# Attention transposes two row blocks behind their scores, seven probability buffers, and the memory features written over the query rows

## Chip, core and metric

The kernel runs on one core of one Trainium2 chip, as one launch. The metric is the device time of that launch in microseconds (us). An engine that a row names PE is TensorE's matmuls, PEld its weight loads, DVE VectorE, ACT ScalarE, POOL GpSimd and SP the engine that only issues transfers here.

## The reference

Three steps run one after the other. Attention has 4 batches, 8 heads, 576 rows and 64 columns per head; the feed-forward steps see 2304 rows of 512.

```python
scores = scale * np.matmul(q, k.transpose(0, 1, 3, 2))
scores = np.where(causal, -1000000000.0, scores)
scores = scores - scores.max(-1, keepdims=True)
a = np.exp(scores)
a /= a.sum(-1, keepdims=True) + 1e-09
local = np.matmul(a, v)
def phi(x):
    return np.where(x > 0, x, np.exp(x) - 1.0) + 1.0
q_p = phi(q)
mem_ret = np.einsum('bhsd,bhde->bhse', q_p, M_prev)
mem_norm = np.einsum('bhsd,bhd->bhs', q_p, z_prev)[..., None] + 1e-06
out = g * mem_ret / mem_norm + (1 - g) * local     # g = sigmoid(beta), one per head
x = ((x @ w1) * (x @ w2)) @ w3 @ w_out             # x: heads side by side, d_ff 1024
y = (sigmoid(x @ w_gate) * (x @ w_val)) @ w_out2   # d_ff 1536
```

## The kernel before, in words

**Attention.** `attention(b, lag)` (L1066) is a generator for one batch. The 576 rows are cut into five blocks of 116, the eight heads into four pairs; step k of its main loop is row block i of pair p, with p, i = k // 5, k % 5. For each step, `s_part` has TensorE multiply a query block with all keys up to the diagonal, for both heads of the pair (L1169; in batches 1 to 3 three matmuls each, over the high and low parts that `split_qk` makes of q and k), and DVE reads the scores out of PSUM, adds the mask and keeps the row extremum (L1174). Block 4 has 580 columns, more than a PSUM bank holds, so it is done in two pieces: the tiles `s{b}_{p}_4_0_*` and `s{b}_{p}_4_1_*`. The pool for scores has two buffers, one for each head, so the matmuls of the second piece wait until DVE has read the first. Then ACT takes the exponential (`e_part`, L137), DVE and POOL scale the rows (`n_part`, L1197 to L1200), and `t_part` has TensorE transpose the finished block `p` (L1230) into PSUM, from where ACT copies it to `pt` or `pq` (L1248). When the five blocks of a pair are transposed, `a_part` multiplies them with v and adds the memory term (L1283 to L1298), and `l_part` copies the result out.

**The memory term.** `load_rest(p)` loads a pair's query rows `qnr` (L1093, 128 x 640), z, v and M. `mem_steps(p)` makes phi of them on DVE, ACT and POOL: `me` = min(q, 0) (L1107), its exponential, phi = max(q + 1, e) into a tile `mphi` (L1110), the product with z, its row sums and their reciprocal (L1112 to L1117), and phi times that (L1121). `qt_part(p)`, called in block 3 of the pair, has TensorE transpose the result (L1267). `load_rest(p + 1)` is called in block 4 of pair p, and `mem_steps(p + 1)` starts with the next pair.

**The lag.** Step k of the loop also asks for the transposes of step k - lag. In batch 0 the lag is LAG0 = 3, in batches 1 to 3 it is LAG. The probability tiles `p` have PB buffers, two of which one step takes. Transposes of blocks 2 and 3 and the first part of block 4, the q transposes and the output of `a_part` share one PSUM buffer (pool `ps_o`, 1024 columns) in batches 1 to 3.

**The feed-forward steps** (`ffn(b)`) fill TensorE between these: names `ab`, `xw`, `gv`, `abp`, `gvp`, `ot` are their outputs in PSUM, `h`, `hg`, `x` their inputs, and `wslot` is a ring of five weight buffers, which SP fills (L450, L453). `drive()` advances the two generators in proportion to their work; attention of batch b + 1 runs beside the feed-forward steps of batch b. Weights are prepared on chip (products, and high and low parts: `wraw`, `wrawl`, `wS`, `wP`), with loads and stores on the same SP queue.

**What sets the order.** From the feed-forward steps on, TensorE's order is that in which the code issues it. DVE, ACT, POOL and SP are ordered ahead of time by a scheduler that simulates the program; each engine then works through its own list in order, and waits where a row's inputs or buffers are not ready.

Of the kernel before, what the change touches and what calls it, by code (L numbers as in the profile page):

```python
# [7 lines left out]
F32 = mybir.dt.float32  # L8
# [10 lines left out]
B, H, S, D = 4, 8, 576, 64  # L19
T = 116  # L20
NT = 5
# [7 lines left out]
F2 = 1536 // 128  # L29
NJ = F1 + F2  # L30
LAG0 = 3
LAG = 1
PB = 5
RING = 5
R64 = 3
P0 = 8
# [27 lines left out]
def tile_attention_memory_ffn(  # L64
# [21 lines left out]
    ap = ctx.enter_context(tc.tile_pool(name="ap", bufs=2))  # L86
# [24 lines left out]
    def lower(share):  # L111
        owed[share] = owed.get(share, 0.0) + share[phase["n"]]
        if owed[share] >= 1.0:
            owed[share] -= 1.0
            return nc.gpsimd
        return nc.vector
# [19 lines left out]
    def act_fn(**kw):  # L136
        ins = nc.scalar.activation(**kw)  # L137
        if act_last:
            tc.add_manual_dep(
                ins.ins,  # L140
                act_last.pop(),
                mybir.DependencyInfo(mybir.DependencyClass.NoSync, mybir.DependencyReason.DATA),
                reason="table order",
            )
        act_last.append(ins.ins.name)
# [221 lines left out]
    def load64(n):  # L367
        if n < len(conv_slots):
            s = conv_slots[n]
            t = fp.tile([128, 512], I64, tag="r64", name=f"r64_{s}", bufs=R64)  # L370
            src = units[s // 2][0][s % 2]
            d = nc.sync.dma_start(out=t, in_=src.rearrange("p a c -> p (a c)"))
            raw64[s] = t
            last["dma"] = d
# [691 lines left out]
    def attention(b, lag):  # L1066
# [22 lines left out]

        def load_rest(p):  # L1090
            if p < NPAIR:
                q_ = ap.tile([128, NT, 2, D], F32, tag="qnr", name=f"qnr{b}_{p}")
                nc.sync.dma_start(out=q_, in_=qn[b, p])  # L1093
                z_ = ap.tile([128, 2, D], F32, tag="z", name=f"z{b}_{p}")
                nc.sync.dma_start(out=z_, in_=zb[b, p])
                v_ = ap.tile([128, NT, 2, D], F32, tag="vs", name=f"vs{b}_{p}")
                nc.sync.dma_start(out=v_, in_=vn[b, p])
                m_ = ap.tile([128, D], F32, tag="ms", name=f"ms{b}_{p}")
                nc.sync.dma_start(out=m_, in_=md[b, p])
                pairs[p] = (q_[:T], v_[:T], m_, z_[:T])  # L1100

        def mem_steps(p):
            q_, _, _, z_ = pairs[p]
            e = ap.tile([T, NT, 2, D], F32, tag="me", name=f"me{b}_{p}", bufs=1)
            phi = ap.tile([T, NT, 2, D], F32, tag="mphi", name=f"mphi{b}_{p}", bufs=1)
            nrm = ap.tile([T, NT, 2], F32, tag="mn", name=f"mn{b}_{p}", bufs=1)
            nc.vector.tensor_scalar(e, q_, 0.0, None, ALU.min)  # L1107
            yield
            act_fn(out=e, in_=e, func=AF.Exp)
            nc.vector.scalar_tensor_tensor(phi, q_, 1.0, e, ALU.add, ALU.max)  # L1110
            yield
            nc.gpsimd.tensor_mul(e, phi, z_.unsqueeze(1).to_broadcast([T, NT, 2, D]))  # L1112
            yield
            nc.vector.tensor_reduce(nrm, e, AX.X, ALU.add)
            nc.vector.tensor_scalar(nrm, nrm, 1e-6, None, ALU.add)
            nc.vector.reciprocal(nrm, nrm)
            nc.vector.tensor_mul(  # L1117
                nrm, nrm, g[:T, 2 * p : 2 * p + 2].unsqueeze(1).to_broadcast([T, NT, 2])
            )
            yield  # L1120
            lower(SHARE_M).tensor_mul(phi, phi, nrm.unsqueeze(3).to_broadcast([T, NT, 2, D]))  # L1121
            qms[p] = phi


        load_qk(0)
        yield 0.0
        load_rest(0)
        yield 0.0 if first else 0.5
        if first:
# [16 lines left out]
        def s_part(p, i, n):  # L1146
            w = T * (i + 1)
            if n == 0:
                ps_ = []
                for hh in range(2):  # L1150
# [4 lines left out]
                    else:  # L1155
                        ps_.append(ap.tile([T, SP], F32, tag="p", name=name, bufs=PB))
                    np_["n"] += 1
# [175 lines left out]
        for k in range(NPAIR * NT + lag):  # L1333
# [3 lines left out]
            if k < NPAIR * NT:  # L1337
                p, i = divmod(k, NT)
                wgt = 0.25 + 0.25 * (i + 1)
                s_part(p, i, 0)  # L1340
                yield wgt
                if i == NT - 1:
                    s_part(p, i, 1)
                    yield 0.0
                if i == 0:
                    mem = mem_steps(p)
                next(mem, None)
                e_part(p, i, 0)
                yield wgt + between(kk % NT)
                e_part(p, i, 1)  # L1350
                yield wgt + between(kk % NT)
                n_part(p, i)
                if i > 0:
                    next(mem, None)
                if i == 3:
                    qt_part(p)
                if i == 0:
                    load_qk(p + 2 if first else p + 1)
                if i == 4:
                    split_qk(p + 1)  # L1360
                if i == 4:
                    load_rest(p + 1)
                yield wgt + between(kk % NT)
                yield wgt + between(kk % NT)
                yield wgt + between(kk % NT)
            while ts:
                yield ts.pop(0)()
            if kk >= 0 and kk % NT == NT - 1:
                p = kk // NT
# [6 lines left out]
    def drive(fg, ag, ftot, atot, frac, most=1):  # L1376
        fd = ad = 0.0
        alive = ag is not None
        for c in fg:
            fd += c  # L1380
            for _ in range(most):
                if not alive or ad / atot >= fd / (ftot * frac):
                    break
                with tc.high_priority(offset=AHEAD[phase["n"]]):
                    w = next(ag, None)
                if w is None:
                    alive = False
                else:
                    ad += w
        while alive:  # L1390
            alive = next(ag, None) is not None
# [16 lines left out]
    def start():  # L1408
        for g in range(NPREP):
            yield from prep(g)  # L1410
# [3 lines left out]
    def chain(first, second):  # L1414
        for c in first:
            if c is not READY:
                yield c
        if second is not None:
            while True:
                if phase["n"] == 0:  # L1420
                    with tc.issue_after(last["dma"].ins):
                        c = next(second)
                else:
                    c = next(second)
                if c is READY:
                    return
                yield c

    a0 = attention(0, LAG0)
    with tc.manual_schedule(engines={mybir.EngineType.SP}):  # L1430
# [6 lines left out]
        for n in range(2, R64):  # L1437
            load64(n)
    atts = [a0] + [attention(b, LAG) for b in range(1, B)] + [None]
    drive(start(), chain(a0, atts[1]), 42.4 * NPREP + 8 * WAIT, ATOT, 1.0, most=9)  # L1440
# [80 lines left out]
```

## Time and profile before

| | us |
|---|---|
| median of 3 runs | 1017.32 |
| lowest and highest | 1014.89 and 1017.90 |
| the profiled execution | 1013.13 |
| its span on the core | 1011.3 |

The profiled execution is 1.8 us longer than its span and 4.2 us shorter than the median. In the rows below, each engine's busy time is followed by its share of the span. A row of waits says which engine waited at which line for what, the total in us, how often, and the longest. A row of a timeline gives the start in us from the start of the span, how long, the instruction, how many of them in a row, and in brackets the idle time ahead of it with what ended that. "Idle before" in the groups of instructions is the same, summed.

### The profile page before, as it was taken

The page shows a single profiled execution, that of the slowest core. Times are in us where ns is not written, and L with a number is a line of the kernel's source. Part 1 is how long each engine was busy: PE and PEld are TensorE (multiplying, and loading weights), DVE is VectorE, ACT ScalarE, POOL GpSimd, SP SyncE. Part 2 cuts the span into 40 slices and gives each one's busy share as a digit, 9 for nine tenths or more (in the row PEclk, how much of TensorE's full clock was granted, in tenths as well). Part 3 has the DMA queues.
Part 4 walks back from the last instruction along what each step waited for, and adds up shares of the span by engine and source line. Part 5 has one row for each costly group of instructions (what it writes and reads, how often), then busy time and mean ns, then how long its engine had stood idle before and what let it go on. Part 6 is the DMA issues. An engine that isn't in the chain of part 4 may idle for free. (4 is left out here: it accounts for less than half of the span.)

```text
span 1011.3 us, 19894 instructions
## 1 busy us (share of the span) xinstructions
PE 982.4 (97%) x7351; PEld 797.9 (79%) x7351; DVE 731.3 (72%) x1702; ACT 596.6 (59%) x1213; POOL 195.0 (19%) x196
## 2 busy tenths in 40 slices
PE   7999999999999999999999999999999999999998
PEld 3556687888999898898977777778777667797776
DVE  6866788777778826777777668988876757737883
ACT  7987787567777735564654545555655545324451
POOL 3454012213000101312200011343111311201110
PEclk9989999999999999999999999999999999999999
DMA  8865799967777249877887576655655556556532
GB/s 293 245 230 192 247 346 310 326 206 254 249 250 247 98 137 380 286 226 238 297 310 261 176 251 240 214 190 184 200 181 178 185 157 204 186 174 246 183 131 79
DMA packets 95642, 227.21 MB, mean 225 GB/s; under 512 B 11192, under 2 KB 39992, under 8 KB 95288
## 3 DMA queue, kind: packets, MB, share of 16 engines
q1 hardware_dynamic: 95544, 225.93, 66.3%
q8 instruction: 58, 0.95, 0.4%
q14 instruction: 40, 0.33, 0.1%
HBM read 164.55 MB, written 61.34 MB: 223 GB/s over the span
## 5 line engine op out<-in xcount | busy, mean ns | idle before, releaser
L532 PEld LDWEIGHTS <-wslot 128*128 128x128 f16 x1680 | 162.9, 98 | 49.7 <-issue 8.3
L1200 POOL TENSOR_SCALAR p<-p,sm,omg 116x116 f32<-116x116 f32 (+4 forms) x100 | 89.0, 895 | 406.2 <-DVE sm L1198 294.9
L521 PE MATMUL gv<-x,wslot 128*128 128x288 f32 (+1 forms) x1152 | 147.5, 290 | 0.2 <-ACT gsb L137 0.2
L521 PEld LDWEIGHTS <-wslot 128*128 128x128 f16 x1152 | 111.1, 98 | 32.1 <-issue 4.5
L532 PE MATMUL gvp<-x,wslot 128*128 128x288 f16 x1008 | 125.2, 286 | 3.6 <-ACT x L180 1.6
L137 ACT ACTIVATE p<-p,sm 116x116 f32<-116x116 f32 (+4 forms) x160 | 93.2, 585 | 46.6 <-DVE sm L1174 46.5
L521 PE MATMUL ot<-hg,wslot 128*128 128x288 f16 (+1 forms) x864 | 118.1, 291 | 0.0
L521 PE MATMUL ab<-x,wslot 128*128 128x288 f32 x768 | 117.2, 302 | 0.5 <-ACT asb L800 0.3
L521 PE MATMUL xw<-h,wslot 128*128 128x288 f32 x768 | 113.0, 300 | 1.7 <-ACT h L721 1.0
L521 PEld LDWEIGHTS ab<-x,wslot 128*128 128x128 f32 x768 | 104.0, 188 | 6.3 <-issue 2.9
L521 PEld LDWEIGHTS xw<-h,wslot 128*128 128x128 f32 x768 | 103.4, 188 | 5.5 <-issue 2.0
L1174 DVE CUSTOM_DVE_ANT_0 p<-s,msk 116x116 f32<-116x116 f32 (+4 forms) x160 | 68.0, 452 | 30.8 <-PE s L1169 26.8
L532 PE MATMUL abp<-x,wslot 128*128 128x288 f16 x672 | 87.1, 286 | 1.3 <-DVE u2ab L603 1.1
L723 DVE TENSOR_TENSOR wslot<-wraw,wslot 128x512 fp32r<-128x512 f32 x76 | 54.9, 725 | 34.7 <-ACT wslot L721 34.4
L521 PEld LDWEIGHTS gv<-x,wslot 128*128 128x128 f32 x576 | 76.4, 188 | 0.5 <-ACT gsb L137 0.5
L1230 PE MATMUL t<-idf,p 116*116 116x116 f32 x480 | 68.7, 272 | 3.3 <-DVE p L1200 2.5
L1230 PEld LDWEIGHTS t<-idf,p 116*116 116x116 f32 x480 | 54.3, 139 | 18.0 <-issue 5.3
L402 ACT ACTIVATE cy<-r 128x512 f32<-128x512 f32 x76 | 51.5, 678 | 13.3 <-DVE wraw L411 2.6
L721 ACT CAST wslot<-wraw 128x512 fp32r<-128x512 f32 x76 | 47.1, 621 | 16.2 <-PE gv L521 7.4
L411 DVE SCALAR_TENSOR_TENSOR wraw<-cy,cr 128x512 int32<-128x512 int32 x76 | 54.2, 740 | 2.6 <-ACT cr L403 2.1
L521 PE MATMUL wps<-wo,wslot 128*128 128x512 f32 x192 | 52.2, 407 | 0.0
L1248 ACT COPY pt<-t 116x696 f32<-116x696 f32 (+2 forms) x74 | 47.5, 650 | 7.4 <-PE t L1230 7.1
(210 smaller groups left out, 1630.0 us busy)
## 6 DMA issues: line engine op xcount, KB each, us to landing
wslot<-k SPq DMA_DIRECT2D x40, 512.0 KB, 4.3
wslot<-ka SPq DMA_DIRECT2D x40, 512.0 KB, 4.4
wrawl<-kf SPq DMA_DIRECT2D x32, 512.0 KB, 6.1
wslot<-kb SPq DMA_DIRECT2D x40, 384.0 KB, 3.5
k<-wslot SPq DMA_DIRECT2D x24, 512.0 KB, 4.7
r<-in_gv_dram SPq DMA_DIRECT2D x24, 512.0 KB, 5.1
kf<-wraw SPq DMA_DIRECT2D x20, 512.0 KB, 3.5
ka<-wS SPq DMA_DIRECT2D x20, 512.0 KB, 4.4
```

The lines of the kernel that those rows point to most:

```text
L137: ins = nc.scalar.activation(**kw)
L402: nc.scalar.activation(out=y, in_=hi, func=AF.Prelu, scale=2.0**-112, alpha=2.0**32)
L411: nc.vector.scalar_tensor_tensor(z, y, 3, tmp["r"], ALU.logical_shift_left, ALU.bitwise_or)
L521: paced["pe"] = nc.tensor.matmul(ps, w[:, wi, blk, :], x[:, xi, cols : cols + n], start=first and part == 0, stop=last and part == 2,)
L532: paced["pe"] = nc.tensor.matmul(ps, w[:, wi, blk + k, :], x[:, xi, k, :], start=not more and k == 0 and part == 0, stop=k == 1 and part == 2,
L721: nc.scalar.copy(dst[:, 0], src)
L723: eng.tensor_sub(dst[:, 1], src, dst[:, 0].bitcast(F32))
L1174: nc.vector.tensor_tensor_reduce(out=ps_[hh][:, c0:c1], in0=os_[hh], in1=msk[:, SP - w + c0 : SP - w + c1], scale=-0.125, scalar=3.0e38 if ...
L1200: lower(SHARE_N).tensor_scalar(ps_[hh][:, :w], ps_[hh][:, :w], sm[:, 6 + hh : 7 + hh], omg[:T, 2 * p + hh : 2 * p + hh + 1], ALU.mult, ALU ...
L1230: nc.tensor.transpose(tp[:T, c : c + T], src[hh][:, j * T : (j + 1) * T], idf[:T, :T])
L1248: nc.scalar.copy(to, got)
```

## The change

LAG goes from 1 to 2 and PB from 5 to 7. The query rows `qnr` have one buffer of their own where they had the two of their pool, and phi is written over them: `mphi` is gone. The transposes that `qt_part` does therefore read `qnr`.

```diff
--- before.py
+++ after.py
@@ -29,8 +29,8 @@
 F2 = 1536 // 128
 NJ = F1 + F2
 LAG0 = 3
-LAG = 1
-PB = 5
+LAG = 2
+PB = 7
 RING = 5
 R64 = 3
 P0 = 8
@@ -1089,7 +1089,7 @@
 
         def load_rest(p):
             if p < NPAIR:
-                q_ = ap.tile([128, NT, 2, D], F32, tag="qnr", name=f"qnr{b}_{p}")
+                q_ = ap.tile([128, NT, 2, D], F32, tag="qnr", name=f"qnr{b}_{p}", bufs=1)
                 nc.sync.dma_start(out=q_, in_=qn[b, p])
                 z_ = ap.tile([128, 2, D], F32, tag="z", name=f"z{b}_{p}")
                 nc.sync.dma_start(out=z_, in_=zb[b, p])
@@ -1102,7 +1102,7 @@
         def mem_steps(p):
             q_, _, _, z_ = pairs[p]
             e = ap.tile([T, NT, 2, D], F32, tag="me", name=f"me{b}_{p}", bufs=1)
-            phi = ap.tile([T, NT, 2, D], F32, tag="mphi", name=f"mphi{b}_{p}", bufs=1)
+            phi = q_
             nrm = ap.tile([T, NT, 2], F32, tag="mn", name=f"mn{b}_{p}", bufs=1)
             nc.vector.tensor_scalar(e, q_, 0.0, None, ALU.min)
             yield
```

The three numbers and the alias move instructions on every engine. Names carry batch, pair, block: `p2_3_4_0` is the probability tile of batch 2, pair 3, block 4, head 0; the last number of a name counts tiles and differs between the two programs.

The order on TensorE, just behind the scores of the last block of batch 2, pair 3. Before:

```order
L1169 MATMUL s2_3_4_1_0_7470<-qkl2_3_6120,qkh2_3_6119 116x290
L1169 MATMUL s2_3_4_1_1_7471<-qkl2_3_6120,qkh2_3_6119 116x290
L521 LDWEIGHTS wslot114_7096
L521 MATMUL ot1_1_0_7426<-hg1_8_6941,wslot114_7096 128x288
L521 LDWEIGHTS wslot114_7096
L521 MATMUL ot1_1_0_7426<-hg1_8_6941,wslot114_7096 128x288
L521 LDWEIGHTS wslot114_7096
L521 MATMUL ot1_1_0_7426<-hg1_8_6941,wslot114_7096 128x288
L1230 MATMUL t2_3_3_0_7484<-idf_80,p2_3_3_0_7356 116x116 x4
L1230 MATMUL t2_3_3_0_7484<-idf_80,p2_3_3_1_7357 116x116 x4
```

With the change:

```order
L1169 MATMUL s2_3_4_1_0_7443<-qkl2_3_6093,qkh2_3_6092 116x290
L1169 MATMUL s2_3_4_1_1_7444<-qkl2_3_6093,qkh2_3_6092 116x290
L521 LDWEIGHTS wslot115_7153
L521 MATMUL ot1_1_0_7406<-hg1_7_6852,wslot115_7153 128x288
L521 LDWEIGHTS wslot115_7153
L521 MATMUL ot1_1_0_7406<-hg1_7_6852,wslot115_7153 128x288
L521 LDWEIGHTS wslot115_7153
L521 MATMUL ot1_1_0_7406<-hg1_7_6852,wslot115_7153 128x288
L1230 MATMUL t2_3_2_0_7461<-idf_80,p2_3_2_0_7244 116x116 x3
L1230 MATMUL t2_3_2_0_7461<-idf_80,p2_3_2_1_7245 116x116 x3
```

Behind the same scores, the transposes of block 2 stand where those of block 3 stood. Those of block 3 now follow 36 matmuls of `ot` later, and those of block 4 six matmuls of `ot` behind those of block 3, where it was 39.

The order on SP around the load of the query rows of batch 3, pair 0, with what each transfer waits for. Before:

```order
L453 DMA wslot94_5763<-k42_134 128x1024 [waits DMAHW4_49,PE_49]
L344 DMA kb34_172<-wP10_5737 128x2048 [waits DMAHW5_49,DVE_49]
L302 DMA wrawl_13_5761<-ko01_177 128x1024 [waits DMAHW6_49]
L1093 DMA qnr3_0_7619<-in_qn_dram 128x640 [waits DMAHW7_49,DVE_49]
L1095 DMA z3_0_7621<-in_zb_dram 128x128 [waits DMAHW0_49,Pool_49]
L1099 DMA ms2_3_6131<-in_md_dram 128x64 [waits DMAHW1_49,PE_49]
L1097 DMA vs2_3_6129<-in_vn_dram 128x640 [waits DMAHW2_49,PE_49]
```

With the change:

```order
L344 DMA ka19_130<-wS25_7347 128x2048 [waits DMAHW0_49,DVE_49]
L302 DMA wrawl_28_7364<-kf26_146 128x1024 [waits DMAHW1_49]
L450 DMA wslot117_7401<-op1_184 128x1536 [waits DMAHW2_49,PE_49]
L1093 DMA qnr3_0_7607<-in_qn_dram 128x640 [waits DMAHW3_49,PE_49,Pool_49]
L450 DMA wslot118_7413<-op1_184 128x1536 [waits DMAHW4_49,PE_49]
L1007 DMA out_0_dram<-osb1_0_1_7320 128x288 [waits DMAHW5_49,Activation_49]
L344 DMA ka24_141<-wS26_7456 128x2048 [waits DMAHW6_49,DVE_49]
```

The load stands some 70 rows further on in SP's list, and waits for PE (the q transposes of pair 3 of batch 2, `qt2_3`) where it waited for DVE.

The order on DVE at the scores of the last block of batch 2, pair 3. Before:

```order
L436 TENSOR_TENSOR wrawl_26_7240<-wrawl_26_7240 128x256
L1200 TENSOR_SCALAR p2_3_3_0_7356<-p2_3_3_0_7356,sm2_3_3_7358,omg_91 116x464
L181 SCALAR_TENSOR_TENSOR wS26_7466<-wrawl_26_7240,wsc_83,wS26_7466 128x1024
L1174 ISA p2_3_4_0_7447,sm2_3_4_7449<-s2_3_4_0_0_7450,msk_81 116x290
L1174 ISA sm2_3_4_7449 116x1
L1174 ISA p2_3_4_1_7448,sm2_3_4_7449<-s2_3_4_0_1_7451,msk_81 116x290
L1174 ISA sm2_3_4_7449 116x1
L1174 ISA p2_3_4_0_7447,sm2_3_4_7449<-s2_3_4_1_0_7470,msk_81,sm2_3_4_7449 116x290
```

With the change:

```order
L436 TENSOR_TENSOR wrawl_26_7229<-wrawl_26_7229 128x256
L1200 TENSOR_SCALAR p2_3_3_0_7331<-p2_3_3_0_7331,sm2_3_3_7333,omg_91 116x464
L1107 TENSOR_SCALAR me3_0_7880<-qnr3_0_7607 116x640
L1174 ISA p2_3_4_0_7421,sm2_3_4_7423<-s2_3_4_0_0_7424,msk_81 116x290
L1174 ISA sm2_3_4_7423 116x1
L1174 ISA p2_3_4_1_7422,sm2_3_4_7423<-s2_3_4_0_1_7425,msk_81 116x290
L1174 ISA sm2_3_4_7423 116x1
L1174 ISA p2_3_4_0_7421,sm2_3_4_7423<-s2_3_4_1_0_7443,msk_81,sm2_3_4_7423 116x290
```

The first operation on the new query rows, `me3_0`, stands between the scaling of block 3 and the reading of the scores of block 4. Before it stood 125 rows ahead of those reads. At six places of batches 1 to 3 the operation stands like this, ahead of the reads of the first piece of block 4 or between them: for the query rows of batch 1 pair 3, batch 2 pairs 0, 2 and 3, and batch 3 pairs 0 and 1.

## Rows read from the trace of the kernel before

**Rows 1.** The page, busy time of each engine, its share of the span, instructions.

```profile
PE 982.4 (97%) x7351; PEld 797.9 (79%) x7351; DVE 731.3 (72%) x1702; ACT 596.6 (59%) x1213; POOL 195.0 (19%) x196
```

**Rows 2.** The view of TensorE's waits: total us, times, longest.

```profile
PE s L1169 <- DVE sm L1174: 6.4, 10, 1.4
...
PE t L1230 <- DVE p L1200: 2.5, 3, 1.5
...
PE xw L521 <- ACT h L721: 1.0, 1, 1.0
PE qt L1267 <- ACT pt L1248: 0.8, 2, 0.4
PE xw L521 <- DVE h L723: 0.7, 1, 0.7
PE t L1230 <- POOL p L1200: 0.6, 1, 0.6
```

**Rows 3.** Timeline of TensorE, four places of batches 1 to 3: transposes and second score pieces.

```profile
121.17 0.58 PE L1230 MATMUL t<-idf,p 116*116 116x116 f32 x4 [1.49 <-DVE p L1200]
...
347.06 0.90 PE L1169 MATMUL s<-qkh 64*116 64x290 f32 x2 [1.16 <-DVE sm L1174]
...
644.00 0.72 PE L1267 MATMUL qt<-idf,mphi 116*128 116x116 f32 x5 [0.35 <-ACT pt L1248]
...
788.72 0.77 PE L1169 MATMUL s<-qkh 64*116 64x290 f32 x2 [0.72 <-DVE sm L1174]
```

**Rows 4.** Timeline of TensorE, batch 2, pair 3, from the q transposes to the second piece.

```profile
585.89 0.66 PE L1267 MATMUL qt<-idf,mphi 116*128 116x116 f32 x5
586.39 2.37 PE L521 MATMUL ot<-hg,wslot 128*128 128x288 f16 x18
588.69 0.39 PE L1169 MATMUL s<-qkh 64*116 64x290 f32 x2
...
590.12 0.68 PE L1169 MATMUL s<-qkh 64*116 64x290 f32 x2
```

**Rows 5.** The view of DMA issues, and line L1093 alone: the query rows.

```profile
qnr<-in_qn_dram SPq DMA_DIRECT2D x16, 320.0 KB, 5.0
...
DMA to landing us min/median/max: 2.9/5.0/7.7
```

**Rows 6.** Groups of DVE instructions, shapes apart: busy us, mean ns, idle before.

```profile
L723 DVE TENSOR_TENSOR wslot<-wraw,wslot 128x512 fp32r<-128x512 f32 x76 | 54.9, 725 | 34.7 <-ACT wslot L721 34.4
...
L176 DVE TENSOR_REDUCE mcol<-wraw 128x1 bf16<-128x512 f32 x36 | 24.4, 679 | 0.0
...
L1174 DVE CUSTOM_DVE_ANT_0 p<-s,msk 116x290 f32<-116x290 f32 x32 | 13.7, 453 | 8.8 <-PE s L1169 5.6 <-PE ot L521 3.2
...
L1107 DVE TENSOR_SCALAR me<-qnr 116x640 f32<-116x640 f32 x16 | 7.8, 485 | 0.1
...
L176 DVE TENSOR_REDUCE x2top<-x 128x1 f32<-128x576 f16 x4 | 3.0, 743 | 0.0
...
L181 DVE SCALAR_TENSOR_TENSOR x<-x,x2s,x 128x576 f16<-128x576 f32 x1 | 0.8, 819 | 0.3 <-ACT x L180 0.3
...
L1036 DVE TENSOR_SCALAR x2back<-wsc,x2s 128x12 f32<-128x12 f32 x3 | 0.7, 228 | 0.1
```

**Rows 7.** The view of SP's waits: the load of the query rows.

```profile
SPq L1093 <- DVE mphi L1110: 8.2, 4, 3.5
```

**Rows 8.** Timeline of ACT: the copy of one transposed block 3 (116 x 928).

```profile
351.04 0.94 ACT L1248 COPY pt<-t 116x928 f32<-116x928 f32 x1 [1.31 <-PE t L1230]
```

**Rows 9.** Engines and TensorE's granted clock in four stretches: us, busy, clock, DMA share, GB/s.

```profile
58.60:64.24 5.64, 3.60 (x15) 1.77 (x14) 4.84 (x20) 5.34 (x14) 4.08 (x6) 1.00 0.80 276
64.24:71.07 6.83, 6.83 (x25) 3.73 (x26) 3.19 (x13) 6.50 (x18) 4.86 (x7) 0.50 0.54 177
...
347.55:350.96 3.41, 3.41 (x17) 3.08 (x18) 3.41 (x9) 1.25 (x2) 1.15 (x1) 0.50 0.40 154
350.96:358.00 7.04, 7.04 (x57) 7.04 (x56) 2.66 (x7) 4.07 (x9) 1.41 (x2) 1.00 0.34 107
```

## The prediction, made before the change was run

> **What bounds the kernel.** I read the page's busy times first. TensorE is busy for 982.4 of 1011.3 us and DVE for 72% of the span [rows 1], so the end is set by TensorE's order of work, and a change can only move the time through the 29 us in which TensorE idles, or through its clock. Next comes the view of what TensorE waits for [rows 2]. The waits that this change aims at are small: transposes that wait for a scaled probability block, 2.5 us on DVE in three places and 0.6 us on POOL in one, and q transposes that wait for ACT to empty the shared PSUM buffer, 0.8 us in two. The largest kind, 6.4 us in ten places, is a score matmul that waits until DVE has read a score buffer. Third is TensorE's timeline at single places: the longest wait of a transpose, 1.49 us at 121.17, a second score piece that waits 1.16 us at 347.06, and a q transposition that waits 0.35 us at 644.00 [rows 3]. Last are the stretches by granted clock: right behind that 1.16 us wait TensorE has a granted clock of 0.50, the lower of its two levels (1.2 of 2.4 GHz), for 3.41 us [rows 9]. A wait can thus cost more than its own length.
>
> **What the lag takes away.** With one more row block between scores and transposes, exponential and scaling have twice the distance. Between the scores of a block and its transposes stood some 30 to 90 TensorE matmuls, now 50 to 160. The largest wait of this kind is 1.49 us, some 12 matmuls of 0.128 us (18 of them take 586.39 to 588.69 in [rows 4]), so all four waits go: -3.1 us (0 to -3.1) [rows 2]. Users of the shared PSUM buffer that stood next to each other are pulled apart in the middle of a pair, and both waits of q transposes go: -0.8 us. The second score piece at 788.72 is now separated from the first by a whole block of the feed-forward step (559 matmuls in the new order): -0.7 us [rows 3].
>
> **What the lag adds.** At the end of a batch no scores come between the last steps, so the transposes of block 3 and of block 4 (first part), which use the same PSUM buffer, stand six `ot` matmuls apart in batches 2 and 3 where 30 and 39 lay between them. Six take 0.77 us by the rate above. The copy that empties the buffer takes 0.94 us [rows 8], with about 0.1 us of hand-over around it, so TensorE waits some 0.3 us twice: +0.6 (0 if ACT is early, 3 if ACT is behind other work).
>
> **Seven probability buffers** cost nothing on an engine. A step takes two, and with lag 2 three steps are alive, so six are needed and a seventh is spare. The operations stay the same in number and shape; writing phi in place changes no duration.
>
> **What the single buffer adds.** This is the main term. Before, the load of a pair's query rows waited only for DVE, and SP lost 8.2 us in four places by it [rows 7]; the first operation on them, `me`, sat with 0.1 us of idle time in all sixteen [rows 6], so the rows were always there. Now the buffer holds phi of the pair before until TensorE has transposed it. The load is issued behind that, lands 2.9 to 7.7 us later, 5.0 in the median [rows 5], and only then can `me` of the next pair run. DVE takes its list in order. At six places `me` stands ahead of the reads of the first score piece of block 4 (front section, the order on DVE), and the second score piece waits for these reads. So TensorE stops there unless its work between the q transposes and the second piece is longer than load, `me` and read together.
>
> That work is short. In the trace before, batch 2, pair 3, the matmul behind the q transposes starts at 586.39 and the second piece at 590.12 [rows 4]; the new order has three more `ot` matmuls between them, 3.9 us from the end of the transposes. Against it stand 0.1 us of hand-over, 5.0 us of load, 0.485 us of `me`, and about 0.38 us until the read of one head is done (it takes 0.453 us and is issued back to back) [rows 6]: 5.96 us. The stall is 2.0 us. The same reckoning for the six places, in the order in which they come, with the distances of the new order 4.25, 4.1, 4.27, 4.35, 3.94 and 3.56 us, and with what else DVE's list holds between `me` and the reads (a `wslot` and an `mcol` operation, 0.725 + 0.679, at the first; a `wslot` at the second; three operations on x2, 0.228 + 0.819 + 0.743, at the fourth) [rows 6], gives 3.1, 2.5, 1.7, 3.3, 2.0 and 2.4 us, 15.0 together. Two of the places had waits already that these swallow: the first lay behind the two waits for `h`, 1.0 + 0.7 us [rows 2], the second is the 1.16 us at 347.06 [rows 3]. Net +12.1 us. With every load at its fastest, 2.9 us, the same sum is 2.9 us gross and 1.5 net; with every load at 7.7 us it is 28.3 net. I take the median, since SP's list shows a weight load right ahead of this one, which shares the transfer engines with it.
>
> One more place: `me` of the last pair of batch 3 stands ahead of DVE work that the next feed-forward block needs. I give it +1.0, between nothing and the 2.4 us of the like place in that batch. In batch 0 the query loads wait for transposes too, but there DVE and POOL are behind TensorE's work anyway and `me` has room: 0, with 2 us either way, about what TensorE's gap in the stretch 58.60 to 64.24 comes to [rows 9].
>
> **The clock.** Behind 1.16 us of waiting came 3.41 us at half clock, behind about 2 us in the stretch 58.60 to 64.24 came 6.83 us [rows 9]; behind the 1.49 us at 121.17 came none. The new stalls are of the length of those that cost clock. Half of 3.41 us is 1.7 us; I count it for three of the six: +5.1, between 0 and twice 6 x 1.7, about 20.
>
> **The sum.** -3.1 - 0.8 - 0.7 + 0.6 + 12.1 + 1.0 + 5.1 = +14.2 us on the profiled execution of 1013.13, so 1027.3. That execution is 4.2 us below the median of the runs; against the median the forecast is 1017.3 + 14.2 = 1031.5, slower by 1.4%.
>
> **Rivals.** (1) *The loads land in time, faster.* It decides at one place: if the query rows land within about 2.9 us behind the q transposes, the stalls shrink to 1.5 us or less, none of them costs clock, and the 1.7 us of half clock behind 347.06 may go too. The sum is then -4.6 + 0.6 + 1.5 = -2.5 without and -4.2 with the clock, or -5.7 without any stall: about 1013. For it speaks the fastest load, 2.9 us; against it the median of 5.0 over sixteen loads. The Trainium skill, "DMA: Bandwidth & Descriptors", section on the anatomy of one DMA (written for the GpSimd path), fits a transfer as 2.0 us plus its bytes over 436 GB/s, which for 327,680 bytes would be an estimate of 2.75 us, this rival's case; by this the trace's fastest row agrees and its median does not, and the measured rows decide. (2) *Gains and stalls cancel, no change.* DVE already waits at some of these places for other work, and loads near 3.5 us leave some 4 us of stalls: about 1017. For it speaks that all terms are parts of a per cent. (3) *Loads late and the clock lost.* SP handles its list in order too: a query load that waits for TensorE holds up the weight loads behind it, and these in turn delay TensorE. With loads at 6 to 7.7 us and half clock after all six stalls the sum is near +33: about 1050. Against it speaks that 7.7 us is the slowest of sixteen loads and 5.0 the median [rows 5]. A case in which the change does nothing to the order is excluded by the listings: the operations do move.
>
> **How the numbers follow.** A measurement of this kernel tells about 0.3%, 3 us, from no change. The forecast (stalls of 6 to 25 us with their clock) has a chance of 0.62, rival 3 0.10, both slower; rival 2 0.13; rival 1 0.15. So faster 0.15, same 0.13, slower 0.72. The predicted time is the forecast's, 1031.5. The range leaves out one in ten on each side: its low end, 1014, takes in rival 2 and the better part of rival 1, its high end, 1046, most loads late with half clock after most stalls. The forecast's own range is 1021 to 1043.
>
> **What would show it.** In the new profile, waits of transposes on DVE and POOL should be gone from TensorE's waits, and those of q transposes on ACT; the wait of score matmuls on DVE's reads should grow from 6.4 to about 18 us, with single ones of 2 to 3 us; `me` should show idle time released by the load of `qnr`, and that load, on SP, should wait for the q transposes. The clock row should show short half-clock stretches behind some of these waits. I am wrong if `me` shows no idle time on its load, or if it does and the second score pieces don't wait; in the first case the loads were faster than their median before, in the second DVE had other slack that I took for none.

## The result and the profile after

The changed kernel takes 1022.36 us (median of 6 runs, 1017.60 to 1024.31), the kernel before 1016.19 us (6 runs, 1014.80 to 1017.90). The ratio is 1.0057, with an interval of 1.0034 to 1.0079: slower by 0.6%, 6.2 us. The forecast was slower by 14.2 us. The profiled execution takes 1021.22 us with a span of 1019.3 us, 8.0 us more span than before.

The profile of the changed kernel, busy times from the page:

```profile
PE 985.6 (97%) x7351; PEld 802.5 (79%) x7351; DVE 735.4 (72%) x1702; ACT 594.6 (58%) x1213; POOL 194.8 (19%) x196
```

Against [rows 1] TensorE is busy 3.2 us longer and idles 4.8 us longer (33.7 for 28.9): together the 8.0. Its waits (total us, times, longest):

```profile
PE s L1169 <- DVE sm L1174: 9.7, 11, 2.3
...
PE abp L532 <- DVE u2ab L603: 2.8, 4, 0.9
PE ab L521 <- DVE wpart L748: 2.6, 3, 1.8
...
PE xw L521 <- ACT x2f L850: 1.0, 1, 1.0
...
PE ot L521 <- DVE hg L723: 0.8, 1, 0.8
PE ot L521 <- DVE hg L181: 0.6, 1, 0.6
PE t L1230 <- ACT pt L1248: 0.6, 2, 0.3
```

Against [rows 2], every wait that the lag aimed at is gone: no transpose waits for a scaled block, no q transposition of batches 1 to 3 for the copy. The two new waits at the batch ends are 0.3 us each, as reckoned. Score matmuls wait 9.7 us for DVE instead of 6.4, although batch 0 has 2.5 us less of that. And there are waits for `wpart`, `u2ab` and `hg` that were small or absent.

The late load is there, in the view of line L1093 (the load: who waited for it, and how long it took) and in SP's waits:

```profile
  DVE me L1107: 19.0, 10
...
DMA to landing us min/median/max: 2.8/4.2/6.2
```

```profile
SPq L1093 <- PE qt L1267: 20.7, 10, 5.2
```

DVE stands still 19.0 us in ten places for the query rows, none before [rows 6]. The load lands 2.8 to 6.2 us after its issue, 4.2 in the median, where the kernel before had 5.0 [rows 5]. Of the 19.0 us, 7.8 lie in batch 0 and 11.2 behind it.

One of the six places, batch 3 pair 0's rows behind batch 2 pair 3, on TensorE and on DVE (start, us, instruction, idle ahead):

```profile
587.55 0.66 PE L1267 MATMUL qt<-idf,qnr 116*128 116x116 f32 x5
...
590.35 0.39 PE L1169 MATMUL s<-qkh 64*116 64x290 f32 x2
...
593.43 0.77 PE L1169 MATMUL s<-qkh 64*116 64x290 f32 x2 [1.22 <-DVE sm L1174]
```

```profile
592.50 0.49 DVE L1107 TENSOR_SCALAR me<-qnr 116x640 f32<-116x640 f32 x1 [3.62 <-DMA qnr<-in_qn_dram]
592.91 0.45 DVE L1174 CUSTOM_DVE_ANT_0 p<-s,msk 116x290 f32<-116x290 f32 x1
593.29 0.08 DVE L1174 DVE_READ_ACCUMULATOR2_ANT sm<- 116x1 f32 x1
```

The q transposes begin at 587.55, `me` starts at 592.50 when its load has landed, the score read follows at 592.91, and the second score piece at 593.43 has waited 1.22 us. At the other places the same piece waited 1.88, 0, 0.57, 2.35 and 1.51 us:

```profile
223.30 0.77 PE L1169 MATMUL s<-qkh 64*116 64x290 f32 x2 [1.88 <-DVE sm L1174]
...
442.05 0.39 PE L1169 MATMUL s<-qkh 64*116 64x290 f32 x1 [0.57 <-DVE sm L1174]
...
479.55 0.77 PE L1169 MATMUL s<-qkh 64*116 64x290 f32 x2 [2.35 <-DVE sm L1174]
...
653.60 0.76 PE L1169 MATMUL s<-qkh 64*116 64x290 f32 x2 [1.51 <-DVE sm L1174]
```

At the first of these places, 223.30, it was not the load that held DVE up. Its rows landed at 219.70, and `me` ran at 221.20 without idle time ahead of it, because DVE was busy with other rows all the while:

```profile
221.20 0.48 DVE L1107 TENSOR_SCALAR me<-qnr 116x640 f32<-116x640 f32 x1
```

At the second place the rows landed at 344.19, `me` followed at 344.57 without waiting for them, and the piece did not wait. So the load stopped DVE, and DVE TensorE, at four of the six places: 0.57, 2.35, 1.22 and 1.51 us.

And TensorE's clock in four stretches right behind such waits (length, busy times of PE, PEld, DVE, ACT, POOL, granted clock, DMA share, GB/s):

```profile
224.60:228.10 3.50, 3.50 (x18) 3.48 (x17) 2.12 (x8) 3.48 (x8) 1.78 (x2) 0.51 0.88 305
480.30:483.90 3.60, 3.60 (x20) 3.40 (x17) 2.23 (x7) 3.28 (x8) 1.43 (x1) 0.55 0.05 19
594.20:598.00 3.80, 3.80 (x35) 3.05 (x33) 3.62 (x6) 3.50 (x8) 1.98 (x1) 1.00 0.17 69
654.40:658.00 3.60, 3.60 (x20) 2.65 (x18) 3.35 (x8) 3.33 (x7) 2.27 (x2) 0.55 0.23 69
```

Behind the waits of 1.88, 2.35 and 1.51 us the granted clock is at the lower level for about 3.4 us (the stretches are cut a little wider, so that their means are 0.51 to 0.55); behind that of 1.22 us it stays full.

### The profile page after: what moved, and what is told of

The parts are those of the page before. It is cut to its first block, busy times and chain, and to the rows that moved or that the text cites. A ratio compares the mean times of both kernels' runs of the same rounds, so it can differ in the third digit from the quotient of the medians.

```text
span 1019.3 us, 19830 instructions
## 1 busy us (share of the span) xinstructions
PE 985.6 (97%) x7351; PEld 802.5 (79%) x7351; DVE 735.4 (72%) x1702; ACT 594.6 (58%) x1213; POOL 194.8 (19%) x196
## 5 line engine op out<-in xcount | busy, mean ns | idle before, releaser
L521 PE MATMUL xw<-h,wslot 128*128 128x288 f32 x768 | 115.3, 304 | 1.0 <-ACT x2f L850 1.0
L521 PEld LDWEIGHTS xw<-h,wslot 128*128 128x128 f32 x768 | 105.5, 191 | 4.7 <-issue 2.3
```

The source lines that it names most:

```text
L521: paced["pe"] = nc.tensor.matmul(ps, w[:, wi, blk, :], x[:, xi, cols : cols + n], start=first and part == 0, stop=last and part == 2,)
```

## The experiments

Two theories stood against each other. A: the cost is the load that waits for the q transposes, holds up DVE and through it TensorE. B: the longer lag itself costs. Each ratio below is against the kernel before, timed on the same chip beside it.

**e1: lag 2 with two buffers for the query rows.**

```diff
-PB = 7
+PB = 6
-name=f"qnr{b}_{p}", bufs=1)
+name=f"qnr{b}_{p}")
```

> Lag 2 and phi in place stay, but the query rows have their pool's two buffers again (six probability buffers instead of seven, to make room). The load of the next pair then waits only for the transposes of the pair before the last. Theory A (the load that waits for the q transposes holds up DVE, and DVE holds up TensorE): DVE's idle time on that load falls from 19.0 us to 0, the second score pieces wait under 2.5 us in batches 1 to 3 (8.2 with the change), the new waits on DVE for wpart, u2ab and hg shrink as well, and the time is 1011 to 1015 us where the kernel before has about 1016. Rival B (the longer lag itself costs, by TensorE's order and the shared PSUM buffer): the time stays at 1020 to 1024. Rival C (the six buffers are too few): transposes or reads wait for buffers, above 1017.

Measured: 1017.44 us, ratio 1.001 (0.9991 to 1.0029): 5 us less than the change, but no gain over before. The waits of TensorE:

```profile
PE s L1169 <- DVE sm L1174: 5.6, 7, 1.5
...
PE abp L532 <- DVE u2ab L603: 3.8, 4, 1.5
PE ab L521 <- DVE wpart L748: 2.1, 2, 1.5
...
PE abp L532 <- DVE u3ab L631: 0.9, 3, 0.4
PE ot L521 <- DVE hg L723: 0.8, 1, 0.8
```

The stalls of the score pieces went as theory A has it: two waits of score matmuls remain in batches 1 to 3, 0.94 us and this one, at the place that had 1.88 us with the change:

```profile
229.50 0.76 PE L1169 MATMUL s<-qkh 64*116 64x290 f32 x2 [1.54 <-DVE sm L1174]
```

So at that place the change had some 0.3 us more, less than `me` itself takes (0.48 us), and the rest is DVE's other work: the piece waits there in e3 and e5 too (1.70 and 2.10 us). The waits for `wpart`, `u2ab` and `hg` did not shrink: they are no work of the load. A explains the cost of the change against e1; that e1 has no gain, 1017.44 where 1011 to 1015 were expected, it does not explain. e1 differs from the kernel before in the lag, in the sixth probability buffer and in phi written in place. No run has phi in place alone, so a small cost of it, or of rival C's six buffers, is not excluded.

**e2: the single buffer alone, with lag 1.**

```diff
-PB = 7
+PB = 5
-LAG = 2
+LAG = 1
```

> Lag 1 and five probability buffers as before, with only the single q buffer and phi in place. Theory A: the cost comes from here, DVE idles 12 to 20 us on the load, score pieces wait at four places where the operation on the new rows stands ahead of their reads, 4 to 6 us together, one or two of them cost a stretch of half clock (1.7 us each), and the waits of transposes of the kernel before (3 us) stay: 1020 to 1028 us. Rival B: the memory part is harmless, 1015 to 1018 us.

Measured: 1029.67 us, ratio 1.0135 (1.0105 to 1.0165), above the stated range. Three views of it, waits of TensorE, users of the load, and the clock in five stretches:

```profile
PE s L1169 <- DVE sm L1174: 8.0, 8, 2.6
...
PE t L1230 <- DVE p L1200: 4.4, 5, 1.6
```

```profile
  DVE me L1107: 19.2, 11
```

```profile
127.00:131.00 4.00, 4.00 (x20) 3.95 (x19) 2.30 (x6) 2.72 (x8) 0.40 (x1) 0.58 1.05 407
144.00:147.50 3.50, 3.50 (x17) 3.50 (x17) 1.15 (x4) 0.36 (x2) 1.11 (x1) 0.51 0.96 288
230.20:237.00 6.80, 6.31 (x31) 5.74 (x32) 3.45 (x10) 4.26 (x9) 2.61 (x2) 0.56 0.61 222
355.90:362.50 6.60, 6.60 (x29) 6.16 (x30) 5.31 (x13) 3.28 (x6) 1.43 (x2) 0.50 0.21 79
457.80:461.50 3.70, 3.70 (x19) 3.37 (x19) 3.67 (x8) 2.81 (x6) 1.45 (x1) 0.54 0.87 304
```

The single buffer alone (with phi in place) is worse than the whole change, by some 8 us (0.8% between the two ratios). DVE loses the same 19 us. With lag 1, though, the scaling that DVE has put off by them is late for the transposes (4.4 us, where before had 2.5), and half clock after batch 0 comes to 23.9 us (2 x length x (1 - clock), summed over the span in steps of 3 us), against 10.2 with the change and 3.4 before. About half of that is time lost where TensorE is busy all through. The lag thus protects the transposes from a DVE that is held up; without that to protect from, no gain of it shows (e1).

**e3: the two tiles of the memory term change roles**, so that the rows are free before the q transposes.

```diff
-            e = ap.tile([T, NT, 2, D], F32, tag="me", name=f"me{b}_{p}", bufs=1)
-            phi = q_
+            phi = ap.tile([T, NT, 2, D], F32, tag="me", name=f"me{b}_{p}", bufs=1)
+            e = q_
```

(min and exponential write `phi`, the product with z overwrites the query rows.)

> The change with the two tiles of the memory term swapped: phi is built in the tile me, and the product with z is written over the query rows, which are then free as soon as DVE has summed them, long before the q transposes. Same memory, same operations. The first operation on a new pair now waits for the transposes directly, without a load between. Theory A (it is the load's 3 to 4.5 us between transposes and that operation that cost): no second score piece waits over 1 us, DVE idles under 3 us on the load, 1011 to 1015 us. Rival D (any operation on DVE that waits for the q transposes stops TensorE, load or not): 1018 to 1023 us.

Measured: 1018.36 us, ratio 1.0023 (1.0003 to 1.0043). Of line L1107, DVE's idle time:

```profile
  PE qt L1267: 2.1, 2
  issue: 1.6, 2
  DMA qnr<-in_qn_dram: 0.6, 1
```

The load is out of the way (0.6 us for 19.0), and what waits for the transposes directly costs 2.1 us. The time is that of e1, not the 1011 to 1015 expected: again no gain against the kernel before. One score piece still waits 1.70 us, at the place where e1 has 1.54.

**e4: the same swap with lag 1.** Edit: LAG = 1 and PB = 5 in e3.

> The swap of e3 with lag 1 and five buffers, as before. Theory A: neither gain nor cost, 1014 to 1018 us; the difference to e3 is what the lag is worth by itself, 2 to 5 us. Rival B: e4 is faster than e3.

Measured: 1019.35 us, ratio 1.0034 (1.0012 to 1.0055): 1 us above e3, where 2 to 5 were expected, with intervals that overlap. The transposes wait again (2.3 us on DVE). e3 and e4 have the same memory part, so this pair says most directly what the lag is worth by itself, and it does not tell that from nothing. e4 is also slower than the kernel before, where 1014 to 1018 were expected: with lag 1 the swapped tiles cost some 3 us without a late load. What costs there was not found.

**e5: the change, with min(q, 0) on POOL.**

```diff
-            nc.vector.tensor_scalar(e, q_, 0.0, None, ALU.min)
+            nc.gpsimd.tensor_scalar(e, q_, 0.0, None, ALU.min)
```

> The change with one operation moved: the first operation on the new query rows (min with 0, 0.485 us on DVE) runs on POOL, so that POOL and not DVE waits for the late load. Theory A (the load costs because DVE stands still in front of the score reads): the second score pieces at batch 2 pairs 2 and 3 and batch 3 pairs 0 and 1, which waited 0.57, 2.35, 1.22 and 1.51 us with the change, wait under 0.4 us each, and the time falls by 3 to 6 us against the change, to 1016 to 1019. Rival E (POOL, standing still with half of the scaled blocks behind it, makes the transposes late): waits of transposes on POOL of 1 us and more, 1020 us or above.

Measured: 1012.38 us, ratio 0.9968 (0.9953 to 0.9982): 0.9%, some 9 us, less than the change, below the 1016 to 1019 of theory A, and faster than before. Of line L1107:

```profile
L1107 POOL TENSOR_SCALAR me<-qnr x16: 1802/1808/2239, 8.4 to 716.8; 116x640 f32<-116x640 f32 x16
...
  DMA qnr<-in_qn_dram: 37.5, 13
```

The operation takes 1.808 us there instead of 0.485, and POOL waits 37.5 us for the rows, twice as long as DVE did; nobody is behind it in a hurry, and no transpose waits for POOL. The score pieces at the four places wait under 0.2 us. One at 132.67 and one at 223.90 wait 1.83 and 2.10 us, behind other work of DVE. The price of the load at the four places was thus set by the engine that waits, not by the wait.

**e6: e1 with three quarters of the scaling on POOL.**

```diff
-SHARE_N = (1.0, 0.5, 0.5, 0.5)
+SHARE_N = (1.0, 0.75, 0.75, 0.75)
```

> Kernel e1 (lag 2, two query buffers, six probability buffers) with three quarters of the scaling of batches 1 to 3 on POOL instead of half. Theory F (what the lag took from the transposes came back as waits of other matmuls because DVE is nearly full in those stretches, 45 to 46 of 50 us between 630 and 680): the waits for u2ab and u3ab (4.3 us in e1) and wpart (2.1) fall by at least 2 us together, and the time is 2 to 4 us below e1's 1017.4. Rival G (those waits come from TensorE's changed order and not from DVE's load): they stay within 1 us of e1's, and so does the time; or POOL (0.9 us per block) becomes late and transposes wait.

Measured: 1012.80 us, ratio 0.9971 (0.9953 to 0.9990), 4.6 us below e1.

```profile
PE s L1169 <- DVE sm L1174: 4.7, 8, 1.3
PE abp L532 <- DVE u2ab L603: 2.3, 3, 1.4
...
PE abp L532 <- DVE u3ab L631: 0.3, 1, 0.3
```

`wpart` has left the list, `u2ab` and `u3ab` fell from 4.7 us in all to 2.6. That speaks for the lag's gain having gone to waits for a DVE that is nearly full there. The stretch from 630 to 680 us, before and in e1 (which is some 3 us later by then, so that the two windows do not hold quite the same work):

```profile
630.00:680.00 50.00, 48.77 (x401) 35.98 (x399) 45.18 (x122) 29.04 (x71) 20.26 (x19) 1.00 0.67 218
```

```profile
630.00:680.00 50.00, 45.62 (x373) 33.55 (x372) 46.51 (x123) 26.79 (x66) 20.69 (x21) 1.00 0.67 225
```

DVE is busy 45.18 of 50 us before and 46.51 in e1. Taking a wait for DVE away at one matmul lets TensorE run up to the next one that needs DVE.

**e7: e1 with lag 1 in batch 3.**

```diff
-    atts = [a0] + [attention(b, LAG) for b in range(1, B)] + [None]
+    atts = [a0] + [attention(b, 1 if b == 3 else LAG) for b in range(1, B)] + [None]
```

> Kernel e1 with lag 1 again in batch 3 alone. If the lag's loss in the stretch of the products abp comes from the lag in that batch: the waits for u2ab and u3ab fall from 4.3 us to about 1.5 and a wait of transposes and q transposes of about 1 us returns, so 1.5 to 3 us less than e1, 1014 to 1016. If those waits come from anything else in e1 (six buffers, phi in place, the two query buffers): they stay at 4 us and the time at 1017 to 1018.

Measured: 1014.26 us, ratio 0.9988 (0.9974 to 1.0003).

```profile
PE ab L521 <- DVE wpart L748: 2.1, 2, 1.5
...
PE abp L532 <- DVE u2ab L603: 1.5, 3, 0.7
```

The waits for `u2ab` fall from 3.8 to 1.5 us with only batch 3's lag undone, those for `wpart` (batch 1) stay at 2.1. The median is 3.2 us below e1's, the ratio 2 us, with intervals that overlap, and e12 below repeats about 1 us of it; so that the longer lag costs time in batch 3 is likely and not shown. A possible reason, not tried by itself, is that the first matmuls of `o` there, 4 us in which TensorE needs nothing new from DVE, start at 676.44 in e1 and at 665.95 before (some 3 us of that is e1's general delay), behind the products that wait and no longer between them.

**e9: the kernel before with three quarters of the scaling on POOL.** Edit: SHARE_N as in e6, in the kernel before.

> The kernel before with three quarters of the scaling of batches 1 to 3 on POOL. With lag 1 a block's transposes come soon behind its scaling: theory F gives transposes that wait on POOL for 1 to 4 us together and DVE waits that shrink by 1 to 2, so 1015 to 1019, not better than before, and the difference between this kernel and e6 is what the lag is worth when POOL is used. If it is faster than before by over 2 us, the lag is not needed for that.

Measured: 1020.24 us, ratio 1.0051 (1.0030 to 1.0071), above the 1015 to 1019 expected.

```profile
PE t L1230 <- POOL p L1200: 4.0, 5, 1.8
```

With lag 1 the transposes wait 4.0 us for POOL. By the ratios the same edit gains some 4 us with lag 2 (e6 against e1) and loses 5 with lag 1: the lag pays when it is used to hide a slower engine.

**e10 to e13: which parts the gain of e5 needs.** e10 is the kernel before with the min on POOL; e11 is e5 with e6's SHARE_N; e12 is e5 with e7's lag 1 in batch 3; e13 is e1 with the min on POOL.

> The kernel before with the min operation on POOL. It tells whether the gain of e5 (1012.4 us) needs the change. If the gain is only 7.8 us of work taken off DVE (16 times 0.485), mostly in batch 0, this kernel is at 1011 to 1014 too. If the change is needed for it (the late load must be waited for by an engine with room, and lag 2 must hide POOL's slower scaling), this kernel stays at 1014 to 1018, with transposes waiting on POOL as in e9.

> e5 with three quarters of the scaling on POOL, the two gains together. If DVE's fullness is what is left behind e5 (u2ab and u3ab waits 4.0 us, score pieces 4 us in batch 1), these waits fall by 2 us or more and the time is 1009 to 1012. If POOL, which already waits 37.5 us for the query rows in e5, becomes late, transposes wait on POOL by 2 us and more and the time is 1013 to 1018.

> e5 with lag 1 in batch 3 alone, as e7 did to e1 (there 3.2 us less, with the waits for u2ab and u3ab down from 4.3 to 1.4). Same here if the two are independent: 1009 to 1011. If POOL's wait for the rows makes batch 3's transposes late at lag 1, they wait on POOL and nothing is won, 1012 to 1015.

> e1 with the min on POOL: e5 without its late load (and with six probability buffers). If the late load still costs something in e5, this is 1 to 3 us faster than e5, 1009 to 1011.5. If POOL hides it fully, the two agree within 1 us. The stretch of half clock in batch 0, absent in e5 and present in e1, e6 and e7, tells whether the single buffer or the operation's engine took it away.

| | us | ratio to before | interval |
|---|---|---|---|
| e10, before + min on POOL | 1020.03 | 1.0027 | 1.0008 to 1.0046 |
| e11, change + min and scaling on POOL | 1012.58 | 0.9953 | 0.9931 to 0.9975 |
| e12, change + min on POOL, lag 1 in batch 3 | 1011.35 | 0.9961 | 0.9939 to 0.9983 |
| e13, two buffers + min on POOL | 1015.00 | 0.9983 | 0.9962 to 1.0004 |

The move to POOL alone loses (e10, above both of its expected ranges), so e5's gain needs something of the change. That it needs the lag is not shown: e10 lacks the single buffer and the other buffers too, and the transposes wait for POOL there only 0.9 us. e11 and e12 are not told apart from e5 by their intervals; their waits moved as expected (`u2ab` 1.5 and 0.8 us for 3.2), their times by about 1 us or less, and e11 falls between its two ranges. e13 missed: it should have been faster than e5, or within 1 us of it, and its median is 2.6 us above it.

The profiled executions tell more when they are cut in two. Ahead of the first matmul of `ab`, where the feed-forward steps begin, every kernel has the same matmuls but for two transposes. The start of that matmul, and from there to the end of the span (us, one execution each):

| | before | change | e1 | e3 | e4 | e5 | e6 | e10 | e13 |
|---|---|---|---|---|---|---|---|---|---|
| start of first `ab` | 117.9 | 117.7 | 121.5 | 123.9 | 122.7 | 114.9 | 122.0 | 120.7 | 119.6 |
| from there to the end | 893.4 | 901.6 | 893.9 | 894.1 | 897.2 | 896.3 | 891.2 | 897.9 | 891.3 |

The change's whole cost lies in the second part, 8.2 us, and e1 takes 7.7 of it back. e5 takes back 5.3 us there and 2.8 in the first part. In the second part it is still 2.9 us longer than the kernel before, and 3.0 shorter in the first: the lead of its median over the kernel before does not show in the part where the lag works. e5 and e13 have equal spans (1011.2 and 1010.9) by luck: with two buffers the second part is 5.0 us shorter and the first 4.7 longer. So e13 does not show that the late load is free on POOL. How much the first part varies from one execution of a kernel to the next is not known; e9, whose edit touches batches 1 to 3 alone, has 120.6 where the kernel before has 117.9.

## Why the prediction was right in sign and wrong in size

**The mechanism** held: the load of the next pair's rows waits for the q transposes, `me` waits for the load, the score reads stand behind `me`, and the second score pieces of block 4 wait for these reads. It happened at four of the six places named. A fifth stalled behind DVE's other work.

**The failed step** is the term of the single buffer, +12.1 us. It was sized with a load of 5.0 us, the median before, at six places, each with a DVE that would be waiting for it. The loads at the six places landed after 2.9 to 4.4 us. The stalls came out at 1.88, 0, 0.57, 2.35, 1.22 and 1.51 us where 3.1, 2.5, 1.7, 3.3, 2.0 and 2.4 were worked out, 7.5 for 15.0. (The rows add up to 2.6 and 3.4 at the second and the fourth.) At the last four the forecast is 0.8 to 1.1 us too long, and 0.65 to 0.85 of that is the error in the load. At the first two the rows were there, 3.0 and 2.9 us behind their issue, before DVE came to them. The first stalled 1.88 us all the same, behind DVE's other work; at the second TensorE had been held up 0.8 us by `hg` on the way. The score waits in batches 1 to 3 rose from 2.4 to 8.2 us. The 2.4 us hold the 0.7 of the piece at 788.72, which the prediction takes off in a term of its own. Less the other 1.7 us, and the 1.7 for `h` that the first stall replaced, the net is 4.8 us for the 12.1. The reason that was given for the median, a weight load right ahead in SP's list, did not make these loads slow.

**The clock**: three of six stalls cost a half-clock stretch, as forecast (5.1 us), but one of the three is the stall at the first place, which was not the load's. What was left out is that the stretch behind 347.06 before, 1.7 us, goes with its wait; TensorE's busy time grew by 3.2 us, not 5.1.

**The lag's own terms** (-3.1, -0.8, -0.7, +0.6) were measured as forecast, each of them, and still no gain shows: e1 has them all and stands at the time of before, and e3 is not told apart from e4. The step that failed here is the rule that a wait that goes is time that goes. The waits for `wpart` (+2.4 us in the changed kernel), `u2ab` (+1.7) and `hg` (+1.4) took their place; e6 speaks for DVE being as late as before for the next matmul. I had named the late engine for the stalls, and not for the gains.

**Batch 0**, priced at 0 with 2 us either way, had 2.5 us fewer waits for score reads, yet the first `ab` starts only 0.2 us earlier: priced at nothing, it came to nothing. (TensorE was busy 1.4 us longer there, which is part of the 3.2.) The +1.0 at the last pair of batch 3 did not show at its place; a wait of that size, of `xw` for `x2f`, came one pair earlier, behind a `me` that had waited 1.7 us for its rows. The errors are of both signs: the load term was 7.3 us too large, the clock 1.9, batch 0's waits 2.5; the new waits on DVE, 5.5 us, were not in the sum. 14.2 - 7.3 - 1.9 - 2.5 + 5.5 = 8.0, the 8.0 measured. That it comes out to the tenth is luck, since waits of 0.9 us and less that came or went are left out. That the sign was right owes something to this too: without the 5.5 us that nobody forecast, this account would leave 2.5 us, which is hard to tell from no change.

**The rivals.** Rival 2 comes nearest: loads near 3.5 us, some 4 us of stalls and a DVE that waits for other work at some of the places are about what the profile shows, and its 1017 is closer to the 1022.36 than 1031.5 is; what it lacked are the new waits on DVE. Rival 1, that the loads land in time, came about at the first two places only. Rival 3, late weight loads, did not: in TensorE's waits none for a weight load grew. The measured time lies at the low end of the forecast's own range (1021 to 1043).

## What to carry to other kernels

Where an engine is nearly full, a wait for it that is removed shows up at its next consumer; count what that engine has to do in the stretch before counting a wait as gained. When a buffer is made single, ask which engine will stand in front of its load, and let one wait that has room: here the same wait, moved from DVE to POOL, gave back 5.3 of 8.2 us behind the first `ab` (e5 against the change), although it was twice as long there. More distance between two steps pays when it is spent on a slower but idle engine for the step between (e6 against e9). When two kernels end at the same time, compare them part by part before calling them equal.

## What the runs showed of the hardware

A wait's length did not settle whether the clock fell behind it. Waits of 1.88, 2.35 and 1.51 us were followed by 3.4 us at the lower level with the change, and one of 1.16 us was before [rows 3, 9]. But none followed on 1.22 us, none on 1.54 us in e1 (at 229.50), and none on 1.84 us with the change, a wait for `wpart`:

```profile
140.26 1.98 PE L521 MATMUL ab<-x,wslot 128*128 128x288 f32 x13 [1.84 <-DVE wpart L748]
```

```profile
140.30:144.00 3.70, 3.70 (x28) 3.70 (x29) 1.83 (x5) 1.10 (x4) 1.14 (x1) 1.00 1.03 380
```

What decides it was not tried.

The granted clock also has a blind spot: it is 1.00 at the start of each profile, where no change of the clock has been recorded yet. The same two score matmuls near 30 us, before and in e5, and the clock of e5 there:

```profile
29.11 0.84 PE L1169 MATMUL s<-qk 64*116 64x348 f32 x2
```

```profile
29.98 1.51 PE L1169 MATMUL s<-qk 64*116 64x348 f32 x2
```

```profile
28.00:37.00 9.00, 9.00 (x25) 4.29 (x22) 7.35 (x16) 9.00 (x22) 5.70 (x6) 1.00 0.54 167
```

A score matmul over 464 columns takes 0.97 to 1.12 us in such a start and 0.98 to 1.12 us in e1's first half-clock stretch (37.4 to 44.2), against 0.55 to 0.64 at full clock. So TensorE starts at the lower level, and by these lengths and the first clock record it stays there until 26.7 us before, 30.1 with the change, 27.2 in e1, 37.3 in e5 and 38.0 in e13 (in each the first 4 to 5 us pass before the first matmul). The stretches in batch 0 that the clock row does show come to 6.8 us before and with the change, 13.7 in e1, and 0 in e5 and e13. Together that is 33.5, 36.9, 40.9, 37.3 and 38.0 us. A kernel without half clock in its row (e5, e11, e12 and e13 have none in batch 0) had more of it at the start instead, and its mean clock looks better than it was; that they gain by a better clock is therefore not shown. What delays the first rise was not tried.
